# A gated mix of a long convolution and a 2-D spectral filter: the first and last FFT stages in 64x64 and 64x32 tiles, a load to contiguous partitions, the convolution's buffers in another place

## The chip, the cores and the metric

One core of one Trainium2 chip runs the kernel. The metric is the time of one execution on the device in microseconds (us), lower is better. Below, PE is TensorE, DVE VectorE, ACT ScalarE, POOL GpSimd, and SP the engine whose queue issues every DMA of this kernel.

## The reference

```python
def _A_ref(u, log_A_real, A_imag, C_real, C_imag, log_dt, D_skip):   # L = 2048, D = 640, N = 128
    dt = jnp.exp(log_dt)
    A = -jnp.exp(log_A_real) + 1j * A_imag
    C = (C_real + 1j * C_imag) * dt[:, None]
    P = jnp.exp((A * dt[:, None])[:, :, None] * pos[None, None, :])
    K = 2.0 * jnp.einsum("dn,dnl->dl", C, P).real
    y = irfft(rfft(u_t, 2 * L) * rfft(K, 2 * L), 2 * L)[:, :, :L]     # along l
    return y + u * D_skip

def _B_ref(x, w_r, w_i):
    return irfft2(rfft2(x) * (w_r + 1j * w_i))                       # over l and d

g = sigmoid((x * gate_w).sum(-1))
return g * _A_ref(x, ...) + (1 - g) * _B_ref(x, ...)
```

The input u is 2048 x 640 in float32, one batch. Each of the 640 channels has its own response K of 2048 samples, made from 128 modes. The output is float32.

## The kernel before

All transforms are matrix products. The transform along l of a column of channels is split in two: stage 1 (`stage1`) works on groups of four channels and is followed by a twiddled stage 2 (`stage2`) over pairs of frequency rows. The 640 channels go in four column groups c of 160. The program has these parts, each with a tag that the planner sees:

- **params** (tag P): small loads, bf16 splits of the modes' parameters on DVE and POOL, stored to `pp_d` and `pm_d` in DRAM.
- **columns** (A): for each c, stage 1 of u (L626, 8 matmuls a block, four groups q; evicted by ACT, L627), the gate's dot products (L678), stage 2 (L636), copies alternately on ACT and DVE (L689), a store to `u_d` in DRAM.
- **responses** (K): 40 blocks of 16 channels; magnitudes (L890, Exp L891), phases (L902, Sin L903), products on POOL (L912) and DVE (L917, L918, twice L920), a sum over modes on PE (L933) and a store to `k_d`.
- **spectral** (F): nine steps over pairs of rows of `u_d`: transposes and products for the transform along d, the filter's products on DVE (L792 to L802), the way back (L811 to L828), a store to `s3e_d`.
- **convolution** (C): for each c, `first` (stage 1 of `k_d`, L626/L627 again), then nine units: stage 2 (L636), products with u (DVE, L986 to L989; u loaded in L1045), the inverse matmuls (L997), a copy (ACT, L999 or L1003) and a store to `s3_d` (L1000, L1004). Then `even` loads te from `s3e_d` (L1010) and `last` loads t3 from `s3_d` (L1024); each has six rounds of short matmuls (L1015, L1031) with evictions of 128x160 that apply the gate (ACT L1017, DVE L1033); the output is stored in two halves (L1035).

A matmul of the program is two MATMUL rows in the trace, since the data are float32.

The program is not issued in the order of the code. Every call is recorded as a unit of a `Plan`; the rows from first to last access of the buffers give the dependences; `order` then simulates the engines with costs per unit (`occ`, `lag`, a DMA rate, a price for a change of PE's tile shape or of ACT's table) and picks on each engine by rank (time to the end of the program, plus a bias by tag, `OPT`). The list that comes out is emitted as it stands. All SBUF buffers are slices of a single tile `sb` and all PSUM buffers are banks of a single tile `ps`, so the semaphores are derived from overlaps of access patterns within these two tiles. `Space` hands out places: from `T.left` on (the responses') and from `T.right` on (the columns', then the filter's). The convolution's working buffers stand in the filter's place. `Banks` hands out PSUM banks in turn.

The t3 load writes each of its four pieces to every fourth partition:

```python
        for y in range(4):
            src = T.s3_d[c, 16 * y:16 * y + 16].rearrange("k (j x a) d -> (k j) x a d", x=2, j=2)
            Y.dma_start(t3[y::4], src, reads=[("s", c, y)] + [("r33", c)] * (y == 2))
```

## Time and profile before

| | |
|---|---|
| median of three runs | 655.2 us (653.47 to 656.76) |
| the profiled execution | 656.0 us, span 654.2 us |
| PE busy | 531.0 us, 81% of the span |
| PE weight loads busy (beside PE) | 373.3 us, 57% |
| DVE busy | 397.9 us, 61% |
| ACT busy | 350.3 us, 54% |
| POOL busy | 178.9 us, 27% |
| moved by DMA | 100.51 MB, mean 154 GB/s |
| mean granted clock of PE | 0.898 |

A row of a profile's view names engine, line, operation, `out<-in` and shapes (partitions x elements, `xN` for N instructions); in brackets stands the idle time ahead of it and what ended it. A row of the waits reads: engine, line, waited for what, then us in total, times, longest. SPq is the queue on SP on which a DMA is issued. The busy times are averages over parts that have different limits, so they are read by stretches of time.

### The profile page before, as it was taken

Reading aid. Unit: us, or ns where it says so; the run is one execution under the profiler, and the core shown is the slowest. Engines: PE = TensorE matmul, PEld = TensorE weight load, DVE = VectorE, ACT = ScalarE, POOL = GpSimd, SP = SyncE. Lnnn points to the kernel's source line nnn. Section 1 sums busy time; section 2 is a strip of 40 time slices with the busy share of each in tenths; the row PEclk is TensorE's granted clock in tenths of the full one; section 3 lists DMA queues with packets and bytes.
Section 4 is the critical chain, followed back from the end, with each engine's and each line's share of the span. In section 5 each row is a group of like instructions: output and inputs, shape, how many; then the busy total and the mean of one; then the engine's idle time right before and its main releaser. Section 6 shows DMA issues by size and latency. Waiting matters only on the chain.

```text
span 654.2 us, 18460 instructions
## 1 busy us (share of the span) xinstructions
PE 531.0 (81%) x7956; PEld 373.3 (57%) x7956; DVE 397.9 (61%) x724; ACT 350.3 (54%) x572; POOL 178.9 (27%) x159
## 2 busy tenths in 40 slices
PE   7578999788989789898999989928669679469354
PEld 7476986466556556666665647817547457345110
...
GB/s 317 303 146 182 217 174 244 153 90 90 106 78 142 99 154 20 139 66 58 58 50 170 225 80 127 316 151 96 208 80 284 258 149 228 215 153 187 214 40 80
DMA packets 54041, 100.51 MB, mean 154 GB/s; under 512 B 4484, under 2 KB 38024, under 8 KB 52680
## 3 DMA queue, kind: packets, MB, share of 16 engines
...
HBM read 60.00 MB, written 39.32 MB: 152 GB/s over the span
## 4 chain that ended last, share of the span: by engine, by line
PE 46%; DVE 25%; DMA 11%; ACT 7%; issue 4%; SPq 1%; POOL 0%; DVEq 0%; ACTq 0%
PE ps L636 11%; PE ps L626 8%; DMA sb<-s_d 7%; PE ps L997 5%; DMA sb<-u_d 5%; PE ps L1015 4%; PE ps L902 4%; DVE sb L920 4%; PE ps L933 3%; PE ps L726 3%; PE ps L1031 3%; ACT sb L891 2%; DVE sb L918 2%; DVE sb L917 2%; PE ps L827 2%
## 5 line engine op out<-in xcount | busy, mean ns | idle before, releaser
L912 POOL TENSOR_TENSOR sb<-sb 128x512 f32<-128x512 f32 x80 | 108.9, 1387 | 100.4 <-ACT sb L903 96.2
L636 PE MATMUL ps<-sb 128*64 128x160 f32 x1056 | 96.5, 326 | 31.6 <-DMA sb<-s_d 16.3
L636 PEld LDWEIGHTS ps<-sb 128*64 128x64 f32 x1056 | 79.7, 144 | 50.5 <-issue 14.5
L626 PE MATMUL ps<-sb 128*64 128x128 f32 x1280 | 88.4, 289 | 5.5 <-DMA sb<-in_t_c 3.8
L626 PEld LDWEIGHTS ps<-sb 128*64 128x64 f32 x1280 | 77.7, 145 | 14.8 <-issue 5.4
L902 PE MATMUL ps<-sb 52*128 52x512 bf16 x480 | 72.4, 395 | 13.0 <-ACT sb L903 6.8
L627 ACT COPY sb<-ps 128x512 f32<-128x512 f32 x80 | 53.6, 673 | 47.1 <-PE ps L626 47.1
L986 DVE TENSOR_TENSOR sb<-ps,sb 128x640 f32<-128x640 f32 (+1 forms) x36 | 28.3, 785 | 74.0 <-PE ps L636 44.1
L1015 PE MATMUL ps<-sb 128*64 128x480 f32 (+1 forms) x96 | 30.5, 716 | 46.8 <-DMA sb<-s_d 41.8
L891 ACT ACTIVATE sb<-ps 128x1024 f32<-128x1024 f32 (+1 forms) x80 | 62.5, 830 | 5.3 <-PE ps L890 5.0
L999 ACT COPY sb<-ps 128x640 f32<-128x640 f32 x32 | 22.3, 695 | 77.0 <-DMA sb<-s_d 35.9
L689 DVE COPY sb<-ps 128x320 f32<-128x320 f32 x32 | 15.5, 489 | 61.6 <-PE ps L636 39.8
L903 ACT ACTIVATE ps<-ps 128x1024 f32<-128x1024 f32 x40 | 40.5, 1012 | 21.7 <-PE ps L902 11.9
L920 DVE TENSOR_TENSOR sb<-sb,ps 128x512 f32<-128x512 f32 x80 | 51.0, 678 | 0.0
L726 PE MATMUL ps<-sb 128*128 128x161 f32 (+3 forms) x280 | 48.6, 316 | 1.5 <-DVE sb L814 1.5
L997 PE MATMUL ps<-sb 64*64 64x160 f32 x1056 | 49.2, 319 | 0.5 <-DVE sb L988 0.5
L902 PEld LDWEIGHTS <-sb 52*128 52x128 bf16 x480 | 24.1, 97 | 41.2 <-issue 28.5
L903 ACT ACTIVATE sb<-ps 128x1024 f32<-128x1024 f32 x40 | 41.3, 1033 | 11.2 <-PE ps L902 11.1
L997 PEld LDWEIGHTS ps<-sb 64*64 64x64 f32 x1056 | 37.6, 141 | 16.3 <-issue 10.2
L726 PEld LDWEIGHTS ps<-sb 128*128 128x128 f32 (+1 forms) x280 | 39.9, 190 | 11.9 <-issue 8.0
L1033 DVE SCALAR_TENSOR_TENSOR sb<-ps,sb 128x160 f32<-128x160 f32 x64 | 20.8, 377 | 41.2 <-issue 27.8
L917 DVE SCALAR_TENSOR_TENSOR sb<-sb,ps 128x512 f32<-128x512 f32 x40 | 27.3, 683 | 30.5 <-ACT ps L903 30.3
...
## 6 DMA issues: line engine op xcount, KB each, us to landing
...
```

The source lines that it names most:

```text
L626: T.P.matmul(p[64 * ri:64 * ri + 64, j, :], src(i + j), e1[ri], start=True, stop=True)
L627: copy(t1v[:, 4 * (q0 + i):4 * (q0 + i) + 16], p.rearrange("p q (j x y) -> p (q j) x y", j=4, y=2))
L636: T.P.matmul(p[64 * j:64 * j + 64, i, 160 * ri:160 * ri + 160], T.w2[:, x, 64 * ri:64 * ri + 64], t1[:, x // 2 if x < 32 else K0 // 2, :, ...
L726: P.matmul(p[:, 161 * i:161 * i + n], lhs(i, part), tab(i)[part][0], start=i == 0, stop=False)
L891: u = S.activation(ef[:, :, c:c + n], p[:, :, :n], AF.Exp)
L902: P.matmul(p[:, h, :], st.pp[l, zz], turns[l, v, s], start=s == 0, stop=s == 2)
L903: u = S.activation(p if o is None else o, p if o is None else p.rearrange("p h (v c) -> p h v c", v=2), AF.Sin, scale=TWO_PI)
L912: G.tensor_tensor(out=y[:, v], in0=e[:, :, 64:96], in1=sc[:, 1 - v], op=ALU.mult)
L917: V.scalar_tensor_tensor(out=xh[:, 1, :, :, 32:64], in0=eh[:, :, :, 32:64], scalar=-1.0, in1=pv[:, 0], op0=ALU.mult, op1=ALU.mult)
L920: V.tensor_tensor(out=xh[:, 0, h].rearrange("p d (y j) -> p d y j", y=2), in0=eh[:, h, :, 0:64].rearrange("p d (y j) -> p d y j", y=2), in ...
L997: P.matmul(q[x:x + 64, j, 160 * i:160 * i + 160], w3[l, pr + i, ri, x:x + 64], t2[l, ri, i, :], start=ri + i == 0, stop=ri == 1 and i == n ...
L1015: P.matmul(p[i:i + 64], T.e3e[:, i:i + 64], te[:, a:a + n], start=True, stop=True)
```

## The change

- **Stage 1** goes from 128x64 tiles of PE to four 64x64 tiles: the table e1 is cut into two 64-row halves without the zeros between them; eight groups q make a block of 32 matmuls of 64 columns into a pair of banks, and two evictions of 128x512. In the columns these are one on ACT and one on DVE, in the convolution both on ACT. The two halves of a column are 24 and 16 groups (`HALVES`).
- **The last stages** go to eight 64x32 tiles: a round is eight matmuls into a pair of banks, and `even` and `last` have three rounds each (three, three and two rows), with six or four evictions of 128x160. They are one generator `final(c)`.
- **t3** is loaded to contiguous partitions, in six pieces (two of 640 KB, four of 320 KB). The load of te has its source's rows in another order, four groups of 32 where there were 128 rows in a row. The output has another layout, two stores of 640 KB for each c, both after the last round; the host's function turns it back.
- **Places**: the convolution's working buffers stand in the responses' place; te, t3, the even rows and the output, and a second set of u and s3 buffers (used from c = 2), stand in the filter's. PSUM: the inverse and stage 2 have a pair of banks each for c = 0 and 1, later the stage 2 has two pairs. `first(c + 1)` and `final(c - 1)` are interleaved with the units of c in the code.
- **The planner** has other costs for DMAs, for small matmuls and for a change of tile shape, and biases by tag in `OPT`.

The lines behind it are numbered differently: L626 becomes L632, L636 L645, L689 L701, L917/L918/L920 L931/L932/L934, L986 to L989 L998 to L1001, L997 L1009, L999 L1011, L1000 L1012, L1010 L1036, both L1015 and L1031 L1028, L1017 L1038, L1024 L1042, L1033 L1045, L1035 L1047, L1045 L1063.

```diff
-OPT = {}
+OPT = {"bias": {"K": -40e3, "A": 3500.0, "P": 30e3, "C": -40e3}, "hold": 600.0, "table": 1000.0, "slack": {"SP": 300.0, "POOL": 0.0, "PE": 300.0}}
...
-                u = plan.unit(name, {"SP": 60, "ACT": 60, "POOL": 600}[name], 0)
+                u = plan.unit(name, {"SP": 500, "ACT": 500, "POOL": 1200}[name], 0)
...
-    sw, tl = opt.get("switch", 90.0), 1294.0
+    sw, tl = opt.get("switch", 160.0), 1294.0
...
+HALVES = ((0, 24), (24, 16))
...
-        T.e1 = [take(128), take(128)]
-        T.e3, T.e3e, T.id, T.one = take(64), take(128), take(128), take(32)
+        T.e1 = [take(64), take(64)]
+        T.e3, T.e3e, T.id, T.one = take(32), take(64), take(128), take(32)
...
-def stage1(T, bank, e1, src, q0, nq, t1, copy):
-
-    t1v = t1.rearrange("p x d y -> p d x y")
-    for i in range(0, nq, 4):
-        p = bank().rearrange("p (q x) -> p q x", q=4)
+def stage1(T, pair, src, q0, nq, t1, copies):
+
+    t1v = t1.rearrange("p x (q h) y -> p h q x y", h=2)
+    for i in range(0, nq, 8):
+        n = min(8, nq - i)
+        p = pair()
         with block(T.R):
-            for j in range(4):
+            for j in range(n):
                 for ri in range(2):
-                    T.P.matmul(p[64 * ri:64 * ri + 64, j, :], src(i + j), e1[ri], start=True, stop=True)
-        copy(t1v[:, 4 * (q0 + i):4 * (q0 + i) + 16], p.rearrange("p q (j x y) -> p (q j) x y", j=4, y=2))
+                    for h in range(2):
+                        l = slice(64 * h, 64 * h + 64)
+                        T.P.matmul(p[64 * ri:64 * ri + 64, h, 64 * j:64 * j + 64], src(i + j)[l], T.e1[ri][l], start=True, stop=True)
+        for h in range(2):
+            q = 2 * (q0 + i)
+            copies[h](t1v[:, h, q:q + 2 * n], p[:, h, 0:64 * n].rearrange("p (q x y) -> p q x y", x=16, y=2))
+        yield
...
-    bank = Banks(R, [0, 1, 2])
+    wide = Banks(R, [0, 3], 2), Banks(R, [0], 2)
+    slim = Banks(R, [2, 5, 6, 7]), Banks(R, [2, 0, 1])
...
+        pair, bank = wide[c // 2], slim[c // 2]
+        for h, (q0, n) in enumerate(HALVES):
...
-            stage1(T, bank, T.e1, lambda q: u[:, q, :], 20 * h, 20, t1, S.copy)
+                Y.dma_start(T.us[-1][:, 0:n], A["u_l"][c + 1, :, q0:q0 + n])
+            zz = T.az()[:, 0:n]
+            G.tensor_tensor(out=zz, in0=T.one.unsqueeze(1).broadcast_to([128, n, 32]),
+                            in1=T.gw[:, c, q0:q0 + n].unsqueeze(2).broadcast_to([128, n, 32]), op=ALU.mult)
+            for _ in stage1(T, pair, lambda q: u[:, q, :], q0, n, t1, (S.copy, V.tensor_copy)):
+                pass
...
 def convolution(T, A, out):
     R, V, G, S, P, Y = T.R, T.V, T.G, T.S, T.P, T.Y
+    z = Space(R, T.left)
+    kp, t1p, w3p = z.pool(2, 24, 64), z.pool(2, 16, 160, 2), z.pool(1, 17, 2, 128)
+    up, wk, t2p, s3p = z.pool(2, 4, 2, 160), z.pool(4, 2, 2, 160), z.pool(2, 2, 2, 160), z.pool(2, 2, 2, 160)
+    assert z.at <= T.right
     z = Space(R, T.right)
-    kp, t1p, w3p = z.pool(2, 20, 64), z.pool(1, 16, 160, 2), z.pool(1, 17, 2, 128)
-    up, wk, t2p, s3p = z.pool(2, 4, 2, 160), z.pool(4, 2, 2, 160), z.pool(2, 2, 2, 160), z.pool(2, 2, 2, 160)
-    z = Space(R, T.left)
-    t1q = z.pool(1, 16, 160, 2)
-    t1p.bases += t1q.bases
-    oep, tep, t3p, otp = z.pool(2, 16, 160), z.pool(1, 16, 160), z.pool(1, 2, 16, 160), z.pool(2, 8, 160)
-    for pool, more in ((up, z.pool(2, 4, 2, 160)), (s3p, z.pool(2, 2, 2, 160))):
-        pool.bases += more.bases
-    b1, b2, bi, bl = Banks(R, [0]), Banks(R, [1, 3], 2), Banks(R, [5], 2), Banks(R, [7])
+    oep, tep, t3p, otp = z.pool(2, 2, 8, 160), z.pool(1, 16, 160), z.pool(1, 2, 16, 160), z.pool(2, 2, 8, 160)
+    more = (up, z.pool(2, 4, 2, 160)), (s3p, z.pool(2, 2, 2, 160))
+    fin = Banks(R, [0], 2)
+    rings = [(Banks(R, [5], 2), Banks(R, [3], 2))] * 2 + [(Banks(R, [6], 2), Banks(R, [2, 4], 2))] * 2
     w3 = w3p()
     for x in range(2):
         Y.dma_start(w3.rearrange("p k r m -> p (k r m)")[:, 2176 * x:2176 * x + 2176], A["t_w3c"][:, 2176 * x:2176 * x + 2176])
     S.activation(T.gate[:, 1, :], T.gate[:, 0, :], AF.Sigmoid, scale=-1.0)
     S.activation(T.gate[:, 0, :], T.gate[:, 0, :], AF.Sigmoid)
-    def first(c):
-        t1 = t1p()
-        for h in range(2):
+    def first(c, t1):
+        for q0, n in HALVES:
             kt = kp()
-            Y.dma_start(kt, T.k_d[c, :, 20 * h:20 * h + 20], reads=[("k", c, q) for q in range(5 * h, 5 * h + 5)])
-            stage1(T, b1, T.e1, lambda q: kt[:, q, :], 20 * h, 20, t1, S.copy)
-        return t1
+            Y.dma_start(kt[:, 0:n], T.k_d[c, :, q0:q0 + n], reads=[("k", c, q) for q in range(q0 // 4, (q0 + n) // 4)])
+            yield from stage1(T, fin if c > 2 else rings[c][0], lambda q: kt[:, q, :], q0, n, t1, (S.copy, S.copy))
     def unit(c, t1, pr, us):
         n = min(2, 17 - pr)
         nl = 128 if pr < 16 else 64
+        bi, b2 = rings[c]
         p = b2()
         with block(R):
             for i in range(n):
...
             S.copy(s3[:, 0, 0], q[:, 0, 0:160])
             Y.dma_start(T.s3_d[c, 33], s3[0:64, 0, 0, :], writes=[("r33", c)])
-    AS = ((0, 3), (3, 3), (6, 2), (8, 3), (11, 3), (14, 2))
-
-    def even(c):
+    AS = ((0, 3), (3, 3), (6, 2))
+
+    def finish(src, w, take):
+        for a, n in AS:
+            p = fin()[:, :, 0:160 * n].rearrange("p j (a d) -> p j a d", a=n)
+            with block(R):
+                for s in range(2):
+                    for x in range(2):
+                        for j in range(2):
+                            l, o = slice(64 * j, 64 * j + 64), 64 * x + 32 * s
+                            P.matmul(p[o:o + 32, j], w(l, x), src(l, x, 8 * s + a, n), start=True, stop=True)
+            for j in range(2):
+                for i in range(n):
+                    take(j, a + i, p[:, j, i])
+            yield
+
+    def final(c):
         te, oe = tep(), oep()
-        Y.dma_start(te, T.s3e_d[c].rearrange("k (r a) d -> (k r) a d", r=4), reads=[("e", k) for k in range(16)] + [("e1",)])
-        for a, n in AS:
-            p = bl()[:, 0:160 * n].rearrange("p (a d) -> p a d", a=n)
-            with block(R):
-                for i in (0, 64):
-                    P.matmul(p[i:i + 64], T.e3e[:, i:i + 64], te[:, a:a + n], start=True, stop=True)
-            for j in range(n):
-                S.activation(oe[:, a + j], p[:, j], AF.Copy, scale=T.gate[:, 1, a + j:a + j + 1])
-        return oe
-
-    def last(c, oe):
-        t3 = t3p()
-        for y in range(4):
-            src = T.s3_d[c, 16 * y:16 * y + 16].rearrange("k (j x a) d -> (k j) x a d", x=2, j=2)
-            Y.dma_start(t3[y::4], src, reads=[("s", c, y)] + [("r33", c)] * (y == 2))
-        for k, (a, n) in enumerate(AS):
-            if k % 3 == 0:
-                ot = otp()
-            p = bl()[:, 0:160 * n].rearrange("p (a d) -> p a d", a=n)
-            with block(R):
-                for x in range(2):
-                    P.matmul(p[64 * x:64 * x + 64], T.e3, t3[:, x, a:a + n], start=True, stop=True)
-            for j in range(n):
-                V.scalar_tensor_tensor(out=ot[:, a % 8 + j], in0=p[:, j], scalar=T.gate[:, 0, a + j:a + j + 1], in1=oe[:, a + j], op0=ALU.mult, op1=ALU.add)
-            if k % 3 == 2:
-                Y.dma_start(out[c, :, a - 6:a + 2], ot)
-
-    t1 = first(0)
+        Y.dma_start(te.rearrange("p a d -> p (a d)"), T.s3e_d[c].rearrange("k (r a) d -> r k (a d)", r=4), reads=[("e", k) for k in range(16)] + [("e1",)])
+        yield from finish(lambda l, x, a, n: te[l, a:a + n], lambda l, x: T.e3e[l, 32 * x:32 * x + 32],
+                          lambda j, a, p: S.activation(oe[:, j, a], p, AF.Copy, scale=T.gate[:, 1, 8 * j + a:8 * j + a + 1]))
+        t3, ot = t3p(), otp()
+        for k0, k1, ys in ((0, 32, (0, 1)), (32, 48, (2,)), (48, 64, (3,))):
+            for j in range(2):
+                Y.dma_start(t3[64 * j + k0:64 * j + k1].rearrange("p x a d -> p (x a) d"), T.s3_d[c, k0:k1, 32 * j:32 * j + 32],
+                            reads=[("s", c, y) for y in ys] + [("r33", c)] * (k0 == 32))
+        yield from finish(lambda l, x, a, n: t3[l, x, a:a + n], lambda l, x: T.e3[l],
+                          lambda j, a, p: V.scalar_tensor_tensor(out=ot[:, j, a], in0=p, scalar=T.gate[:, 0, 8 * j + a:8 * j + a + 1], in1=oe[:, j, a], op0=ALU.mult, op1=ALU.add))
+        for j in range(2):
+            Y.dma_start(out[c, j], ot[:, j])
+
+    t1 = [t1p() for _ in range(4)]
+    for _ in first(0, t1[0]):
+        pass
     for c in range(4):
-        nxt = first(c + 1) if c < 3 else None
-        us = {}
+        if c == 2:
+            for pool, x in more:
+                pool.bases = pool.bases + x.bases
+        side = [first(c + 1, t1[c + 1])] if c < 3 else []
+        if c:
+            side.append(final(c - 1))
         for g in (0, 4, 8, 16, 12):
             gn = min(4, 17 - g)
             nl = 128 if g < 16 else 64
...
             Y.dma_start(u[:nl, 0:gn], T.u_d[c, :nl, g:g + gn], reads=[("u", c, g + i) for i in range(gn)])
             for pr in range(g, g + gn, 2):
                 n = min(2, g + gn - pr)
-                unit(c, t1, pr, u[:nl, pr - g:pr - g + n])
-        oe = even(c)
-        last(c, oe)
-        t1 = nxt
+                unit(c, t1[c], pr, u[:nl, pr - g:pr - g + n])
+                for x in side:
+                    next(x, None)
+        for x in side:
+            for _ in x:
+                pass
+    for _ in final(3):
+        pass
```

Three places in the order of the instructions. First, DVE about the end of the columns (L689 is the copy behind stage 2, L693 the gate's sum that stands behind the last dot product, L743 the first operation of the filter). Before:

```order
L689 COPY sb<-ps 128x320 x9
L693 TENSOR_REDUCE sb<-sb 128x64
L689 COPY sb<-ps 128x320 x7
L917 SCALAR_TENSOR_TENSOR sb<-sb,ps 128x16x32
L918 TENSOR_TENSOR sb<-sb,ps 128x16x32
L920 TENSOR_TENSOR sb<-sb,ps 128x512 x2
L698 COPY sb<-ps 32x16 x4
L743 TENSOR_TENSOR sb<-sb 128x640
```

After (L635 is a stage 1 eviction, L952 belongs to a finished pair of responses):

```order
L635 COPY sb<-ps 128x16x16x2
L701 COPY sb<-ps 128x320
L931 SCALAR_TENSOR_TENSOR sb<-sb,ps 128x16x32
L932 TENSOR_TENSOR sb<-sb,ps 128x16x32
L934 TENSOR_TENSOR sb<-sb,ps 128x512 x2
L635 COPY sb<-ps 128x16x16x2 x2
L701 COPY sb<-ps 128x320 x2
L705 TENSOR_REDUCE sb<-sb 128x64
L952 TENSOR_TENSOR sb<-sb 128x8
L701 COPY sb<-ps 128x320 x2
```

Before, one response (of 40) stands on DVE ahead of the filter's first operation; after, responses are woven into the columns, and eight are done there. At the other end of the filter, ten responses stood behind the last L801 on DVE before, and none stands behind the last L815 (the same operation) after.

Second, SP's queue at the end of the program, with the semaphores that each DMA waits for (DMAHW names are other DMAs). Before:

```order
L1024 DMA sb<-s_d 32x5120 [waits DVE_49,DMAHW4_49,PE_49,Activation_49]
L1024 DMA sb<-s_d 32x5120 [waits DMAHW7_49,DMAHW5_49]
L1024 DMA sb<-s_d 32x5120 [waits DMAHW2_49,DMAHW1_49]
L1035 DMA out<-sb 128x1280 [waits DVE_49]
L1000 DMA s_d<-sb 128x4x160 [waits DMAHW0_49]
L1024 DMA sb<-s_d 32x5120 [waits DMAHW3_49,DMAHW0_49,PE_49]
L1035 DMA out<-sb 128x1280 [waits DVE_49] x2
```

After:

```order
L1042 DMA sb<-s_d 32x5120 [waits DMAHW2_49,DMAHW3_49,DMAHW1_49,PE_49]
L1042 DMA sb<-s_d 32x5120 [waits PE_49]
L1042 DMA sb<-s_d 16x5120 [waits DMAHW7_49,DMAHW6_49]
L1042 DMA sb<-s_d 16x5120
L1012 DMA s_d<-sb 128x4x160 [waits DMAHW5_49,Activation_49]
L1047 DMA out<-sb 128x1280 [waits DVE_49] x2
L1042 DMA sb<-s_d 16x5120 [waits DMAHW5_49,DMAHW0_49]
L1042 DMA sb<-s_d 16x5120 [waits DMAHW1_49]
L1047 DMA out<-sb 128x1280 [waits DMAHW2_49,DVE_49]
L1047 DMA out<-sb 128x1280 [waits DMAHW3_49,DVE_49]
```

The t3 load no longer waits for DVE and ACT, and its pieces of 16 partitions come last.

Third, PE at the end. Before:

```order
L997 MATMUL ps<-sb 64x160 x16
L1031 MATMUL ps<-sb 64x320 x2
L1015 MATMUL ps<-sb 64x480 x4
L1015 MATMUL ps<-sb 64x320 x2
L1015 MATMUL ps<-sb 64x480 x4
L1015 MATMUL ps<-sb 64x320 x2
L1031 MATMUL ps<-sb 64x480 x4
```

After (L1028 is the matmul of both last stages):

```order
L1009 MATMUL ps<-sb 64x160 x16
L1028 MATMUL ps<-sb 32x320 x8
L1028 MATMUL ps<-sb 32x480 x16
L1028 MATMUL ps<-sb 32x320 x8
L1028 MATMUL ps<-sb 32x480 x16
L1028 MATMUL ps<-sb 32x320 x8
```

Behind the last inverse stood one round of column 2 and twelve of column 3; after, one and six.

More of the change, by code (lines that the diff above doesn't have):

```diff
@@ L55, in _tables @@
     kr[K0, 1] = co[32]
-    e1 = np.zeros((2, 4, 32, 4, 32))
-    for r in range(4):
-        e1[:, r, :, JR[r], :] = kr[:32].transpose(1, 2, 0)
-    e1 = e1.reshape(2, 128, 128)
+    e1 = np.zeros((2, 2, 2, 32, 2, 32))
+    for r in range(2):
+        e1[:, :, r, :, r, :] = kr[:32].transpose(1, 2, 0)[:, None]
+    e1 = e1.reshape(2, 128, 64)
     kr = kr[:32].reshape(64, 32)
-    e3 = np.zeros((64, 2, 2, 32))
-    for j in range(2):
-        e3[:, j, j, :] = kr
-    e3e = np.zeros((32, 4, 4, 32))
-    for r in range(4):
-        e3e[:, r, JR[r], :] = kr[32:64]
+    e3 = np.tile(kr, (2, 1))
+    e3e = np.zeros((2, 2, 32, 2, 32))
+    for x in range(2):
+        e3e[:, x, :, x, :] = kr[32:64]
     one = np.tile(np.eye(32), (4, 1))
     c1 = np.concatenate([
-        e1[0], e1[1], e3.reshape(4, 32, 64).swapaxes(0, 1).reshape(128, 64), e3e.reshape(128, 128), np.eye(128), one,
+        e1[0], e1[1], e3, e3e.reshape(128, 64), np.eye(128), one,
         np.repeat([-1.0, 1.0], 64)[:, None], np.repeat([1.0, -1.0], 64)[:, None],
@@ L292, in call @@
                 else:
-                    t = max(40, a[2].free_size() * 4 / 2.4 * rows * cols / 16384)
+                    t = max(20, a[2].free_size() * 4 / 2.4 * rows * cols / 16384)
                 u.occ += t
@@ L298, in call @@
                 if name == "ACT":
-                    fix = 143 if any(isinstance(k.get(x), AP) for x in ("scale", "bias")) else 39 if op == "copy" else 52
+                    fix = 155 if any(isinstance(k.get(x), AP) for x in ("scale", "bias")) else 42 if op == "copy" else 60
                     u = plan.unit(name, 0.833 * n + fix, 115)
@@ L328, in order @@
             follow[v].append(u)
-    land = lambda u: u.occ + u.lag if u.size is None else u.occ + 2100 + u.size / 330.0
+    land = lambda u: u.occ + u.lag if u.size is None else u.occ + 1300 + u.size / 300.0
+    near = {"DVE": 120, "ACT": 115, "POOL": 0, "PE": 0, "SP": 0}
+    for u in units:
+        u.cost = 45.0 if u.eng == "PE" and any(v.eng != "PE" for v in u.pre) else 0.0
     for u in reversed(units):
-        u.tail = max((v.tail + (u.occ if v.eng == u.eng and u.size is None else land(u) + LAT[v.eng]) for v in follow[u]), default=land(u))
+        u.tail = max((v.tail + (u.occ + near[u.eng] if v.eng == u.eng and u.size is None else land(u) + LAT[v.eng]) for v in follow[u]), default=land(u))
     bias = opt.get("bias", {})
@@ L376, in order @@
             if u.mode != mode:
-                s += sw / 2
+                s = max(s, free[e] + sw)
                 mode = u.mode
-                free[e] = s + u.occ + sw / 2
             else:
-                free[e] = s + u.occ
+                s = max(s, free[e] + u.cost)
+            free[e] = s + u.occ
         elif u.table and u.table != table:
@@ L392, in order @@
         if u.size is not None:
-            dma = max(dma, s + u.occ) + u.size / opt.get("bw", 330.0)
-            done = dma + 2100
+            dma = max(dma, s + u.occ + 700) + u.size / opt.get("bw", 300.0)
+            done = dma + 450
         out.append(u)
         for v in follow[u]:
-            t = s + u.occ if v.eng == e and u.size is None else done + LAT[v.eng]
+            t = s + u.occ + near[e] if v.eng == e and u.size is None else done + LAT[v.eng]
             est[v] = max(est[v], t)
@@ L500, in body @@
         R.tag = "A"
-        Y.dma_start(c1[:, 0:256], A["t_c1"][:, 0:256])
+        Y.dma_start(c1[:, 0:128], A["t_c1"][:, 0:128])
         columns_head(T, A)
-        Y.dma_start(c1[:, 256:nc1], A["t_c1"][:, 256:nc1])
+        Y.dma_start(c1[:, 128:nc1], A["t_c1"][:, 128:nc1])
         R.tag = "P"
@@ L668, in columns @@
                 T.us.append(T.au())
-                Y.dma_start(T.us[-1], A["u_l"][c + 1, :, 20 * h:20 * h + 20])
-            zz = T.az()
-            G.tensor_tensor(out=zz, in0=T.one.unsqueeze(1).broadcast_to([128, 20, 32]),
-                            in1=T.gw[:, c, 20 * h:20 * h + 20].unsqueeze(2).broadcast_to([128, 20, 32]), op=ALU.mult)
-            stage1(T, bank, T.e1, lambda q: u[:, q, :], 20 * h, 20, t1, S.copy)
+                Y.dma_start(T.us[-1][:, 0:n], A["u_l"][c + 1, :, q0:q0 + n])
[4 more added lines that the diff above has]
+                pass
             p = bank()[:, 0:64]
             with block(R):
-                for q in range(20):
+                for q in range(n):
                     x = 32 * (q % 4)
-                    P.matmul(p[x:x + 32], zz[:, q, :], u[:, q, :], start=q < 4, stop=q > 15)
+                    P.matmul(p[x:x + 32], zz[:, q, :], u[:, q, :], start=q < 4, stop=q >= n - 4)
             S.copy(T.lg[:, 2 * c + h, :], p)
@@ L696, in columns @@
             P.matmul(p[32 * r:32 * r + 32], T.one, T.lr, start=True, stop=True)
-    for r, x in enumerate((slice(31, 15, -1), slice(32, 48), slice(15, None, -1), slice(48, 64))):
-        V.tensor_copy(T.gate[32 * r:32 * r + 32, 0, :], p[32 * r:32 * r + 32, x])
+    for r in range(4):
+        l, a = slice(32 * r, 32 * r + 32), 8 * r
+        V.tensor_copy(T.gate[l, 0, 0:8], p[l, 31 - a:23 - a if r < 3 else None:-1])
+        V.tensor_copy(T.gate[l, 0, 8:16], p[l, 32 + a:40 + a])
 def spectral(T, A):
@@ L1037, in convolution @@
-    t1 = first(0)
-    for c in range(4):
-        nxt = first(c + 1) if c < 3 else None
-        us = {}
+    AS = ((0, 3), (3, 3), (6, 2))
[4 more added lines that the diff above has]
+                for s in range(2):
+                    for x in range(2):
+                        for j in range(2):
[5 more added lines that the diff above has]
+            yield
```

21 lines of the change are left out of this document (10 added, 11 removed).

## The prediction

> **What bounds the kernel now.** I read the stages first: the busy time of each engine in the stretches params and columns (to 120), responses beside the filter (to 400), convolution (to 607), end. The last row is the first 20 us alone. The columns are stretch, PE, PEld, DVE, ACT, POOL, granted clock, DMA share, GB/s.
>
> ```profile
> 0.00:120.00 120.00, 98.32 (x1549) 84.86 (x1551) 52.71 (x93) 61.18 (x107) 34.84 (x31) 0.92 0.65 227
> 120.00:340.00 220.00, 199.97 (x3075) 133.30 (x3075) 207.20 (x350) 171.25 (x262) 115.84 (x106) 0.98 0.28 87
> 340.00:400.00 60.00, 55.24 (x988) 35.23 (x978) 33.93 (x67) 49.78 (x73) 28.14 (x23) 0.97 0.48 156
> 400.00:421.00 21.00, 21.00 (x466) 17.99 (x466) 16.36 (x30) 10.05 (x13) 0.07 (x1) 1.00 0.77 259
> 421.00:607.00 186.00, 135.52 (x1858) 98.25 (x1852) 81.81 (x169) 52.12 (x103) 0.00 (x0) 0.84 0.57 184
> 607.00:655.00 48.00, 20.90 (x52) 3.66 (x51) 5.89 (x18) 5.92 (x17) 0.00 (x0) 0.53 0.29 103
> 0.00:20.00 20.00, 16.13 (x282) 15.49 (x284) 1.15 (x3) 9.15 (x16) 5.21 (x8) 1.00 0.92 331
> ```
>
> Up to 340 DVE is the bound, 207 of 220 us; from 340 to 400 it is PE, 55 of 60. From 400 to 421 PE is never idle; after 421 it is busy 136 of 186 us and no other engine is busier, so something stops them all. The waits of 400 to 607 (us in total, times, longest) and the chain there say what:
>
> ```profile
> DVE sb L986 <- PE ps L636: 44.1, 21, 6.1
> ACT sb L999 <- DMA sb<-s_d: 35.9, 4, 13.0
> PE ps L1015 <- DMA sb<-s_d: 32.3, 3, 13.5
> DVE sb L989 <- DMA sb<-s_d: 30.9, 3, 14.0
> DVE sb L986 <- DMA sb<-s_d: 28.3, 3, 12.7
> ```
> ```profile
> by line: PE ps L636 17.1%; PE ps L997 16.8%; DMA sb<-s_d 16.7%; DMA sb<-u_d 11.3%; PE ps L626 10.5%; PE ps L1015 8.2%; PE ps L1031 4.2%; DVE sb L987 3.5%; DVE sb L986 3.0%; DVE sb L1033 2.1%; SPq L1024 1.7%; issue 1.6%; PE ps L933 1.1%; DVE
> 421.19 6.52 DMA sb<-u_d
> 427.79 4.17 DMA sb<-s_d
> ```
>
> ACT's copy L999 and DVE's products L986 and L989 don't read what the t3 load (sb<-s_d, L1024) brings, yet they wait for it, three or four times each, up to 14 us; and t3 itself waits for the u load before it. On the chain of these 207 us the t3 loads are 16.7% and the u loads 11.3%, 58.0 us. The first stop:
>
> ```profile
> 423.73 1.33 PE L997 MATMUL ps<-sb 64*64 64x160 f32 x32
> 432.11 0.69 ACT L999 COPY sb<-ps 128x640 f32<-128x640 f32 x1 [8.58 <-DMA sb<-s_d]
> 432.14 0.82 DVE L986 TENSOR_TENSOR sb<-ps,sb 128x640 f32<-128x640 f32 x1 [10.18 <-DMA sb<-s_d]
> ```
>
> ACT and DVE go on within 0.03 us of each other. The last unit ends at 607; what follows is a chain of loads and short rounds:
>
> ```profile
> 607.04 0.69 ACT L999 COPY sb<-ps 128x640 f32<-128x640 f32 x1 [3.61 <-PE ps L997]
> 617.12 1.87 PE L1015 MATMUL ps<-sb 128*64 128x480 f32 x4 [9.49 <-DMA sb<-s_d]
> 619.02 0.96 ACT L1017 ACTIVATE sb<-ps,sb 128x160 f32<-128x160 f32 x3 [11.28 <-PE ps L1015]
> 634.19 1.87 PE L1031 MATMUL ps<-sb 128*64 128x480 f32 x4 [1.91 <-DMA sb<-s_d]
> 649.49 0.68 DVE L1033 SCALAR_TENSOR_TENSOR sb<-ps,sb 128x160 f32<-128x160 f32 x2 [1.44 <-PE ps L1031]
> ```
>
> PE stands for 9.5 us, and then each round (matmul, evictions, matmul, ...) is in series: 17 us of L1015, 17 of L1031, the output's landing.
>
> **The change, part by part.** The sum is made against the profiled execution's own span, 654.2 us (656.0 with what lies around it, 0.8 above the median of 655.2).
>
> *The hand-over to the convolution* now stands at its first product:
>
> ```profile
> 400.81 0.82 DVE L986 TENSOR_TENSOR sb<-ps,sb 128x640 f32<-128x640 f32 x1
> L917 DVE SCALAR_TENSOR_TENSOR sb<-sb,ps 128x512 f32<-128x512 f32 x40 | 27.3, 683 | 30.5 <-ACT ps L903 30.3
> L918 DVE TENSOR_TENSOR sb<-sb,ps 128x512 f32<-128x512 f32 x40 | 27.1, 678 | 0.0
> L920 DVE TENSOR_TENSOR sb<-sb,ps 128x512 f32<-128x512 f32 x80 | 51.0, 678 | 0.0
> L902 PE MATMUL ps<-sb 52*128 52x512 bf16 x480 | 72.4, 395 | 13.0 <-ACT sb L903 6.8
> L933 PE MATMUL ps<-sb 128*32 128x64 f32 x2560 | 45.0, 221 | 0.9 <-POOL sb L912 0.6 <-issue 0.4
> ```
>
> A response costs DVE 0.683 + 3 x 0.678 = 2.72 us and PE at least (72.4 + 45.0)/40 = 2.9. In the new order eight of the 40 are done on DVE in the columns, where DVE was busy 53 of 120 us, against one. So 7 x 2.72 = 19 us leave the stretch behind: 207.2 + 33.9 - 19 = 222, and at the pace of 120 to 340 (207.2/220) that is 236 us, not 280. Against this: the params' loads (2.56 MB) go ahead of the first u load on SP, 7.7 us at 331 GB/s; the columns' PE loses about 20 us of stage 1 and gains 7 x 2.9 = 20; I let the filter begin 5 us later. All responses are now done ahead of the last filter step, so its own chain of PE, DVE and POOL lies bare: 10 us (estimate; DVE was idle 26 of the 60 us in 340 to 400). The loads of w3, k and u for the convolution, now with places of their own, are 4.8 MB, 14.5 us at 331 GB/s, half of it covered: 8. 120 + 5 + 236 + 10 + 8 = 379, so **-22** (-33 if hole and loads are covered and the filter starts on time; -6 if the hole is 26).
>
> *The t3 load.* Contiguous partitions end the false waits: in the built program the new load holds up only the last stage's matmuls, and waits for the stores that it reads and for the matmuls that free its place. Of the 58.0 us I take 40 as gone: the t3 part, 34.6, whole, and little of the u part, since u loads still come through the same queue: **-40** (-35 to -58).
>
> *First stage.* A block of 16 rows stood at 1.09 us between other work, in a run at 4.59/5 = 0.92:
>
> ```profile
> 398.25 1.09 PE L626 MATMUL ps<-sb 128*64 128x128 f32 x16
> 72.17 4.59 PE L626 MATMUL ps<-sb 128*64 128x128 f32 x80
> 130.16 1.11 PE L933 MATMUL ps<-sb 128*32 128x64 f32 x64
> 423.73 1.03 PEld L997 LDWEIGHTS ps<-sb 64*64 64x64 f32 x32 [0.24 <-ACT sb L627]
> ```
>
> A new block has twice the groups in 64 rows of 64 columns. The nearest matmuls are L933's, 64 rows of 64 columns in 1.11 us; the nearest tile is L997's, whose 32 rows of 160 columns (1280 columns for each of four tiles) took 1.33 us, the same 1.0 ns a column as the 1024 columns for each of two tiles in 1.09, so four 64x64 tiles do work side by side. After 400 some 29 old blocks (31.6 us) become 15 new (16.7): **-15**. The other end is zero: at L997's 1.03/32 us a weight load, 64 loads take 2.06 us, as much as two old blocks.
>
> *Last stages.* Six rounds become three of the same columns in twice the tiles. At full clock:
>
> ```profile
> 589.54 1.03 PE L1015 MATMUL ps<-sb 128*64 128x480 f32 x4
> 592.92 0.76 PE L1015 MATMUL ps<-sb 128*64 128x320 f32 x4
> ```
>
> 36 rounds (24 x 1.03 + 12 x 0.76 = 33.8 us) of the body become 18: **-17** (0 if the eight tiles work four at a time). The evictions stay 16 of 128x160 on the same engines, beside other work. Some 11 more changes of tile shape in the convolution at the 0.24 us that stood ahead of L997 above: **+3**.
>
> *What is given back in the body.* Units of column 0 and 1 have one stage 2 pair of banks where two alternated, so the next unit's matmuls wait for L986 and L987 (0.8 us each, beside an inverse of 1.33 us): 18 units that may lose up to 1.1 us, **+8** (0 to +20). And the same 39.7 MB go through in 160 us, 248 GB/s where the fullest stretch had 331 at a DMA share of 0.92, so loads queue: **+14** (0 to +25). The body, 400.8 to 606.9: -40 - 15 - 17 + 3 + 8 + 14 = **-47**, 206 to 159 us (the ends add to -12 and -78; PE's own work, about 129 us, is the floor).
>
> *The end.* After the last inverse now stand one round of column 2 and three + three of column 3, still at half clock (0.53). A round of three rows: 1.87 us of matmuls and six evictions (2 x 0.96), and the single pair of banks makes these serial, so some 3.9; of two rows 1.33 + 1.4. That is 1.3 + 2 x 10.5 = 22, then two output loads of 640 KB where one was (4.7 us from the last eviction to the span's end): 6, and 2 us of starts: 30.5 against 47.3, **-16** (-6 to -22). The t3 load is hidden under the even rows' three rounds: in the trace the last loads start right behind the copy of 607.04 and release PE at 617.12, some 9.4 us; the rounds ahead take 11.8.
>
> *At nothing:* the evictions split to ACT and DVE in the columns (DVE busy 53 of 120), the gate's extra four copies, the 24/16 halves.
>
> Sum: -22 - 47 - 16 = -85, span 569, executed 571, median **571** within its spread.
>
> **The rivals.**
> *The te load on few engines.* The even rows' load (L1010, 1.31 MB) had 128 rows on both sides; its source is now four groups of 32. If the queue spreads a load by its outermost count, four DMA engines carry it: 331/0.92/16 = 22.5 GB/s each, 14.6 us where 16 take 3.6, and all that is queued behind on those four is late by 11 us. Four loads, half of it hidden by units: +22, **593** (615 with none hidden). The trace has no load with such a source, neither for nor against. The Trainium skill, DMA: Bandwidth & Descriptors, section "Why a DMA increments its semaphore by 16 and not by 1", states such a rule: the engines used are the largest number up to 16 that divides the outermost counts of both sides. By that rule it is four here; no trace of this case shows it yet.
>
> *Small tiles no faster.* Weight loads bound stage 1 (2.06 us a block) and eight tiles go four at a time: -15 and -17 vanish, the rounds at the end double (+10), the columns keep their time (+7): **620**. Against it: L997's columns above.
>
> *All chain waits vanish,* loads hidden: -58 in place of -40, +14 and +8 gone: **531 to 545**. Against it: u and s loads still share one queue and 39.7 MB.
>
> *Slower:* the te load comes down to one engine, 58 us each at 22.5 GB/s, in front of t3 and u on SP. Four such loads pay back the 85 us once each holds up the chain for more than 21 us; wholly exposed, 4 x 55 more, **790**, half hidden 680. For it: nothing but that the shape is untried; against it: the outer count is four.
>
> **How the numbers follow.** 0.52 for the forecast (its own ends 552 to 592), 0.29 for te on four engines, 0.08 for the small tiles, 0.08 for all waits gone, 0.03 for slower. The range 540 to 613 holds all of the first two but their edges. Within 0.5% (3.3 us), about what a measurement of this kernel can tell from no change, needs mishaps that add to 85: 0.02; faster 0.95, slower 0.03.
>
> **What would show it.** Right: no ACT or DVE wait on sb<-s_d; stage 1 blocks of 64 rows near 1.1 us; rounds of 16 rows near 1.0 at full clock; the first convolution product near 379; the end near 30 us behind the last inverse; te landing some 4 us after issue. Wrong: te landing at 14 us or more with the units behind it waiting (second rival); 2 us blocks (third); a first product after 390, or DVE waiting for stage 2 throughout columns 0 and 1, would break the first or the given-back terms.

## The result, and the profile after

The changed kernel takes 653.8 us (median of 20 runs, 648.5 to 664.6) against 656.1 before: a ratio of 0.994 (0.991 to 0.997). Executions fall into a faster and a slower state; the ratios, and the times of the experiments, are those of the faster one. The change gains 0.6%, where 571 us and a range of 540 to 613 were forecast. The profiled execution has a span of 648.5 us. Its stages, with the columns of the table before (stretch, PE, PEld, DVE, ACT, POOL, granted clock, DMA share, GB/s); the last three rows are the convolution's body, first product to last inverse, of before and of after, and the end of after:

```profile
120.00:340.00 220.00, 201.06 (x3083) 135.25 (x3081) 204.37 (x351) 175.06 (x263) 119.19 (x107) 0.97 0.32 101
400.00:421.00 21.00, 8.69 (x228) 6.75 (x217) 5.84 (x10) 3.64 (x5) 0.00 (x0) 0.82 0.57 170
421.00:607.00 186.00, 121.64 (x2396) 83.73 (x2396) 81.36 (x166) 53.58 (x105) 0.00 (x0) 0.83 0.69 173
400.80:607.00 206.20, 155.72 (x2304) 115.45 (x2302) 97.37 (x197) 62.17 (x115) 0.00 (x0) 0.86 0.60 192
386.00:599.00 213.00, 140.27 (x2807) 98.64 (x2806) 95.04 (x187) 60.29 (x115) 0.00 (x0) 0.84 0.70 178
599.00:649.00 50.00, 16.16 (x112) 2.46 (x110) 6.58 (x22) 5.58 (x17) 0.00 (x0) 0.56 0.53 129
```

PE has 15 us less to do in the body, and the body is 7 us longer. PE is idle there for 73 us; between 400 and 421, where it never stood still before, it works 9 of 21. The first product comes at 386.2 (400.8 before, 379 forecast), and the end still takes 50 us (47 before, 30 forecast). The waits and the longest stop say what took the place of the t3 load:

```profile
ACT sb L1011 <- DMA s_d<-sb: 68.8, 8, 25.5
PE ps L632 <- ACT sb L1011: 32.5, 4, 18.9
DVE sb L998 <- DMA sb<-u_d: 22.9, 2, 21.4
```
```profile
436.42 0.57 SPq L1036 DMA_DIRECT2D sb<-s3e_d  x1
...
442.83 0.38 SPq L1012 DMA_DIRECT2D s_d<-sb  x1
...
447.79 23.20 SPq L1012 DMA_DIRECT2D s_d<-sb  x2
...
469.91 0.69 ACT L1011 COPY sb<-ps 128x640 f32<-128x640 f32 x1 [25.45 <-DMA s_d<-sb]
470.65 1.98 PE L632 MATMUL ps<-sb 64*64 64x64 f32 x64 [18.95 <-ACT sb L1011]
471.71 0.82 DVE L998 TENSOR_TENSOR sb<-ps,sb 128x640 f32<-128x640 f32 x1 [21.43 <-DMA sb<-u_d]
...
530.54 16.55 SPq L1063 DMA_DIRECT2D sb<-u_d  x2
```
```profile
460.00:468.00 8.00, 0.00 (x0) 0.00 (x0) 0.00 (x0) 0.00 (x0) 0.00 (x0) 0.50 0.25 76
```

No unit waits for t3 any more. ACT's copy L1011 waits for the stores of s to land and free its buffers, 68.8 us in eight stops. In the stop shown, the te load (L1036) was issued at 436.42; by the trace's DMA records its packets ran from 440.9 to 466.6, and the store that the copy waits for was issued behind it, at 442.83. PE stands behind the copy, and DVE waits for a u load. SP's queue stands too: of the 23.2 us of the two stores at 447.79 the first issue takes 5.6 us, and then the queue waits 17.2 us for ACT's copy. The longest single issue is the first of the two u loads at 530.54, 16.1 us, again behind a te load. In eight microseconds of the stop no engine works and the DMA share is 0.25, as much as 4 of 16 DMA engines (the last row).

### The profile page after: what moved, and what is told of

It is laid out like the page before. It is cut to its first block, busy times and chain, and to the rows that moved or that the text cites. A ratio compares the mean times of both kernels' runs of the same rounds, so it can differ in the third digit from the quotient of the medians.

```text
span 648.5 us, 21440 instructions
## 1 busy us (share of the span) xinstructions
PE 495.0 (76%) x9428; PEld 340.0 (52%) x9428; DVE 412.3 (64%) x748; ACT 336.8 (52%) x552; POOL 183.4 (28%) x159
## 5 line engine op out<-in xcount | busy, mean ns | idle before, releaser
L645 PE MATMUL ps<-sb 128*64 128x160 f32 x1056 | 97.4, 320 | 17.1 <-DVE sb L999 8.3
L632 PE MATMUL ps<-sb 64*64 64x64 f32 x2560 | 55.4, 244 | 51.6 <-ACT sb L1011 32.5
L645 PEld LDWEIGHTS ps<-sb 128*64 128x64 f32 x1056 | 74.0, 139 | 37.4 <-DVE sb L999 13.5
L632 PEld LDWEIGHTS ps<-sb 64*64 64x64 f32 x2560 | 49.9, 156 | 62.1 <-ACT sb L1011 35.3
L1011 ACT COPY sb<-ps 128x640 f32<-128x640 f32 x32 | 22.3, 697 | 108.4 <-DMA s_d<-sb 68.8
L1009 PE MATMUL ps<-sb 64*64 64x160 f32 x1056 | 54.6, 326 | 25.6 <-ACT sb L1011 20.3
L635 ACT COPY sb<-ps 128x512 f32<-128x512 f32 x60 | 42.7, 776 | 50.8 <-PE ps L632 50.3
L998 DVE TENSOR_TENSOR sb<-ps,sb 128x640 f32<-128x640 f32 (+1 forms) x36 | 28.2, 784 | 61.1 <-PE ps L645 38.1
L1009 PEld LDWEIGHTS ps<-sb 64*64 64x64 f32 x1056 | 40.2, 145 | 43.4 <-ACT sb L1011 26.4
L1028 PE MATMUL ps<-sb 64*32 64x480 f32 (+1 forms) x384 | 38.1, 667 | 30.8 <-DMA sb<-s3e_d 14.0
L917 ACT ACTIVATE ps<-ps 128x1024 f32<-128x1024 f32 x40 | 40.4, 1010 | 24.0 <-PE ps L916 16.5
L1045 DVE SCALAR_TENSOR_TENSOR sb<-ps,sb 128x160 f32<-128x160 f32 x64 | 19.9, 376 | 50.3 <-issue 33.5
L934 DVE TENSOR_TENSOR sb<-sb,ps 128x512 f32<-128x512 f32 x80 | 51.1, 679 | 0.0
L740 PE MATMUL ps<-sb 128*128 128x161 f32 (+3 forms) x280 | 50.4, 325 | 0.0
L740 PEld LDWEIGHTS ps<-sb 128*128 128x128 f32 (+1 forms) x280 | 41.4, 197 | 11.7 <-issue 6.5
L917 ACT ACTIVATE sb<-ps 128x1024 f32<-128x1024 f32 x40 | 41.3, 1034 | 9.5 <-PE ps L916 9.0
L1000 DVE TENSOR_TENSOR sb<-sb 128x320 f32<-128x320 f32 (+1 forms) x36 | 16.8, 467 | 44.6 <-PE ps L1009 44.4
L947 PE MATMUL ps<-sb 128*32 128x64 f32 x2560 | 43.8, 220 | 0.0
```

The costliest lines, as they stand in the source:

```text
L632: T.P.matmul(p[64 * ri:64 * ri + 64, h, 64 * j:64 * j + 64], src(i + j)[l], T.e1[ri][l], start=True, stop=True)
L635: copies[h](t1v[:, h, q:q + 2 * n], p[:, h, 0:64 * n].rearrange("p (q x y) -> p q x y", x=16, y=2))
L645: T.P.matmul(p[64 * j:64 * j + 64, i, 160 * ri:160 * ri + 160], T.w2[:, x, 64 * ri:64 * ri + 64], t1[:, x // 2 if x < 32 else K0 // 2, :, ...
L740: P.matmul(p[:, 161 * i:161 * i + n], lhs(i, part), tab(i)[part][0], start=i == 0, stop=False)
L917: u = S.activation(p if o is None else o, p if o is None else p.rearrange("p h (v c) -> p h v c", v=2), AF.Sin, scale=TWO_PI)
L934: V.tensor_tensor(out=xh[:, 0, h].rearrange("p d (y j) -> p d y j", y=2), in0=eh[:, h, :, 0:64].rearrange("p d (y j) -> p d y j", y=2), in ...
```

## The experiments

Ratios are against the kernel before on the same chip (656 to 659 us); intervals are 95%.

**te: in four, in two groups, and in the kernel before.** In te_four each te load is four loads of 32 partitions at the same place of the queue:

```diff
-        Y.dma_start(te..., T.s3e_d[c].rearrange("k (r a) d -> r k (a d)", r=4), ...)
+        for r in range(4):
+            Y.dma_start(te[32 * r:32 * r + 32]..., T.s3e_d[c, :, 16 * r:16 * r + 16].rearrange("k a d -> k (a d)"), ...)
```

te_two has two loads `te[64 * r:64 * r + 64]` from `"k (r a) d -> r k (a d)", r=2`. before_te_groups gives only the new source, `"k (r a) d -> r k (a d)"`, to the kernel before. All other instructions keep their order in all three.

> The changed kernel with the te load cut into four loads of 32 partitions (same place in the queue, same order of everything else). Theory A, te was carried by four DMA engines and what queued behind it on them (stores of s, loads of u) stopped the units: the stretches with a DMA share near 0.25 vanish, ACT's copy L1011 no longer waits 10 to 25 us for s_d stores, and the time falls from 654 to 570 to 595. Theory B, the volume of transfers or the two s buffers stop the units: the stops stay and the time is above 635.

> The changed kernel with te in two loads of 64 partitions, whose source has two groups outside instead of four. Theory A (the outermost count sets the number of engines): two engines, a DMA share near 0.13 in the stops, and each te about twice as long (some 30 us alone), so four times 15 to 25 us more: 710 to 750. Theory B: no change within 10 us of 654.

> The kernel before with nothing changed but the te load's source, in four groups of 32 rows (the even rows' result is then of other rows). Theory A: each te takes 15 us or more on four engines and delays t3 and u behind it: 655 becomes 690 to 730. Theory B: within 1% of 655.

te_four: 607.3 us, 0.925 (0.921 to 0.929). te_two: 695.3, 1.059 (1.050 to 1.069). before_te_groups: 714.8, 1.089 (1.085 to 1.094). The first row is the wait of te_four that was 68.8 above, the other two are stretches within stops of te_two:

```profile
ACT sb L1011 <- DMA s_d<-sb: 24.7, 6, 8.1
```
```profile
420.00:428.00 8.00, 0.00 (x0) 0.00 (x0) 0.00 (x0) 0.00 (x0) 0.00 (x0) 0.50 0.13 54
645.00:650.00 5.00, 0.00 (x0) 0.00 (x0) 0.00 (x0) 0.00 (x0) 0.00 (x0) 0.50 0.13 53
```

The dose answers: four groups outside give a share of 0.25, two give 0.13, 32 give no such stop. From its first to its last packet a te load takes 21 to 26 us with four groups (the changed kernel), 28 to 38 with two, 7 to 10 in te_four and 5 to 7 in the kernel before. Against te_four, four groups cost some 46 us (653.8 to 607.3) and two cost 88 (695.3, less than the 710 to 750 expected); in the kernel before, four cost 59. Theory A holds. The Trainium skill, DMA: Bandwidth & Descriptors, section "Why a DMA increments its semaphore by 16 and not by 1", has the rule (the largest number up to 16 that divides both outermost counts), and the trace agrees with it. te_four missed its range of 570 to 595, so more was wrong.

**The t3 load alone.** The kernel before, with `t3[32 * y:32 * y + 32]` for `t3[y::4]` and e3's rows in the matching order (`e3.reshape(128, 64)`); the same order on all engines.

> The kernel before with nothing changed but the t3 load, to contiguous partitions (the rows of the table e3 in the matching order). If the false waits on t3 are worth what the prediction put on them, 40 us go: 610 to 622. If other waits stand right behind them, the time is 635 to 650.

589.8 us, 0.900 (0.895 to 0.904): 66 us, better than the whole change, and more than the 40 forecast. Its body (first row) and end:

```profile
402.00:548.00 146.00, 142.39 (x2316) 107.35 (x2312) 98.05 (x198) 62.72 (x116) 0.00 (x0) 1.00 0.90 272
548.00:588.00 40.00, 15.92 (x50) 2.99 (x48) 5.90 (x18) 5.49 (x17) 0.00 (x0) 0.66 0.44 123
```

PE is busy 142 of 146 us, and for the same matmuls it needs 13 us less than before (155.7): it no longer stops, and its granted clock is 1.00, not 0.86. So a stop costs its own length and then some clock. The changed kernel shows it at one stop: in the idle stretch from 460 to 468 the granted clock was 0.50, and the block of stage 1 behind it (470.65) took 1.98 us, where another run's block took 1.16 (row 60.18 below). With the t3 load settled, the rest of the change, without the te load, costs 17 us (589.8 to 607.3).

**The planner's part.** t3_planner is before_t3_contiguous with the new costs and biases; te_four_oldplan is te_four with those of before.

> The kernel before with the contiguous t3 load and the new planner (costs, biases), old tiles and places. te_four with all the rest of the change is 17 us slower than the contiguous t3 load alone (607 against 590). If the planner's order is what costs (theory P), this one is 600 to 610 as well. If the order is good by itself (responses into the columns, first product earlier by 15 us as in te_four), it is 570 to 582.

> te_four with the planner of before (costs, no biases), new tiles and places. Theory P: 590 or less. If tiles and places cost and the planner gains, it is 615 to 630.

626.8 us, 0.953 (0.948 to 0.957), and 642.8, 0.975 (0.970 to 0.979): neither theory. By the ratios the new order costs 35 us on the old tiles and gains 33 on the new ones, so an order fits the kernel that it was set for. In t3_planner the first product comes at 375, but responses then run on beside the convolution: DVE has 123 us in the body, not 98, and the body is 210 us long.

```profile
375.00:585.00 210.00, 189.22 (x3105) 130.47 (x3103) 123.45 (x240) 104.98 (x164) 25.43 (x20) 0.91 0.65 196
```

**Buffers, and t3 in pieces of 16 partitions.** In te_four_early `if c == 2:` for the second buffers becomes `if c == 1:`, and `rings` has its first entry once, its second three times. In te_four_t3 the pieces `(0, 32, (0, 1)), (32, 48, (2,)), (48, 64, (3,))` become `(0, 32, (0, 1)), (32, 64, (2, 3))`. t3_pieces16 goes the other way: in before_t3_contiguous each piece is two loads of 16 partitions.

> te_four with the second pair of u and s buffers and the two pairs of banks for stage 2 from column 1 on instead of column 2. Theory B (two s buffers and one pair of banks hold the units of columns 0 and 1, where ACT's copy waits for stores): one of these two columns is freed, 607 becomes 594 to 600. Otherwise it stays within 4 us of 607.

> te_four with t3 in pieces of 32 partitions only (four a column in place of two of 32 and four of 16). In the trace's DMA records a 20480-byte packet of t3 took 0.97 us to partitions a stride apart, 1.4 us to 32 contiguous partitions and 2.2 us to 16. Theory D (the transfers' own time is the bound, because few contiguous partitions take data slowly): 16 packets a DMA engine come down from 2.2 to 1.4 us, 12 us less, 594 to 600. Otherwise 603 to 611.

> The kernel before with contiguous t3 in eight pieces of 16 partitions a column in place of four of 32, all else in the same order. Theory D (few contiguous partitions take data slowly): 32 packets a DMA engine go from 1.4 to 2.2 us, 25 us more transfer time; the convolution there has PE busy 141 of 145 us and a DMA share of 0.91, so the transfers become the bound and 590 becomes 600 to 612. If the packets' times in the other runs came from what else was under way, it stays at 588 to 594.

te_four_early: 635.2, 0.963 (0.957 to 0.969); its body is 9 us shorter than te_four's (169 against 178), but the first product comes at 411 instead of 386, and the end is 55 us. So it tells nothing clear of theory B. te_four_t3: 592.5, 0.902 (0.896 to 0.908); the planner's list is also another one there. t3_pieces16: 616.9, 0.939 (0.936 to 0.943), with all other instructions in the same order: by the ratios 26 us more for the same bytes. Mean durations of the t3 packets (20480 bytes each, 512 a run), from the trace's DMA records:

```
kernel                  partitions of a piece     mean us   the last 32 of the run
before                  32, every fourth          0.98      0.89
before_t3_contiguous    32 in a row               1.46      1.36
te_four_t3              32 in a row               1.48      1.51
te_four                 32 and 16 in a row        1.75      2.26 (pieces of 16)
t3_pieces16             16 in a row               2.32      2.02
```

Theory D holds: at the end of the run, with little else under way, the three kinds stand in the same order (0.89, 1.36 to 1.51, 2.02 to 2.26). The Trainium skill, SBUF — State Buffer, section "Door 1: The DMA port swizzle (why `[64,N]` ≈ `[32,N]`)", has it as the number of the 16 ports that the partitions reach. By its table that is 16 for every fourth partition, 8 for 32 in a row and 4 for 16 in a row; the three durations go that way. The body of te_four_t3 and its end:

```profile
384.00:539.00 155.00, 128.98 (x2778) 93.28 (x2774) 91.35 (x176) 59.97 (x115) 0.00 (x0) 0.97 0.81 226
539.00:589.00 50.00, 24.55 (x151) 3.65 (x144) 9.89 (x32) 5.57 (x17) 0.00 (x0) 0.51 0.68 192
```

**The end.** t3_second_place: te_four_t3 with the last column's t3 in the first buffer of t1, no longer used. one_te: that, with the te load for column 0 only. final_on_pool: t3_second_place with te loads and output stores from POOL's queue. out_held: t3_second_place with column 2's output stores behind the last store of s. out_held_te: that, with the last te in a buffer of k.

```diff
-        t3, ot = t3p(), otp()
+        t3, ot = t3p() if c < 3 else Pool(R, [t1p.bases[0]], (2, 16, 160))(), otp()
...
+    for j, ot in held:                                       # out_held: column 2's
+        Y.dma_start(out[2, j], ot[:, j]).pre[stores[3]] = 1
```

> te_four_t3 with a place of its own for the last column's t3 (the first buffer of t1). In te_four_t3 the t3 loads of column 3 waited on SP for the last matmuls of column 2, and the last store of s stood behind them (544 ready, 554 issued). If this is what made the end 49 us where 30 were forecast: 592 becomes 574 to 582. If the transfers' volume made it, it stays within 4 us.

> t3_second_place with the te loads and the output stores issued from POOL's queue, which is idle in the convolution, in place of SP's; the stores of s and the loads of t3 and u on SP no longer stand behind them. If the order on the one queue costs, another 5 to 15 us go; if the transfers themselves are the bound, no change within 4 us.

> t3_second_place with the te load for column 0 only (the other columns use the same rows, 3.9 MB less). If the transfers' time still bounds the convolution, 3 x 32 packets of 0.73 us an engine, 18 us, go in part: 8 to 18 us less than t3_second_place. If PE and its evictions bound it, 0 to 5.

> t3_second_place with the output stores of column 2 held back on SP until the last store of s is issued; the order is otherwise the same. In t3_second_place the copy of the last unit was done at 542.4 and its store issued at 554.2, behind those output stores, which wait for DVE; it then took 8.6 us to land behind their 1.3 MB. If SP's order makes the end long: the store goes out some 8 us earlier and lands some 3 us faster, 594 becomes 582 to 588. If the transfers' volume makes it, the end stays at 50 us and the time within 4 us.

> out_held with a place of its own for the last column's te as well (in the buffers of k, no longer used), so its load needn't wait for column 2's matmuls nor stand on SP ahead of the last stores of s. If SP's order in the last 50 us is what is left, the time falls below out_held by 4 to 10 us; else no change within 4 us, or what the new order of the whole list gives.

t3_second_place: 594.4, 0.906 (0.900 to 0.911), no gain. final_on_pool: 613.5, 0.934 (0.928 to 0.940), worse; in its profiled execution (622.4, 9 us above that) the end takes 35 us, the shortest here, but the first product comes at 399 and the body takes 187. one_te: 576.2 (one of its two runs, the profiled one), against 588.7 to 596.4 for t3_second_place. Its list is another one from the filter on, too: between the two profiled executions (588.7 and 576.2) 5.5 us go ahead of the first product and 5.5 in the body (152.5 to 147.0), where two of the three loads left out had stood. So the transfers' time may bound a part of the body; it is not shown clear of the order. out_held: 589.1, 0.897 (0.894 to 0.900), 6 us by the ratios; out_held_te: 584.0, 0.888 (0.884 to 0.893), the fastest here with all its loads, beating both kernels and, narrowly, the t3 load alone. Here is out_held's end:

```profile
543.12 0.69 ACT L1011 COPY sb<-ps 128x640 f32<-128x640 f32 x1 [6.18 <-DMA s_d<-sb]
...
551.85 0.37 SPq L1012 DMA_DIRECT2D s_d<-sb  x1
554.86 1.77 PE L1028 MATMUL ps<-sb 64*32 64x480 f32 x2 [4.02 <-DMA sb<-s3e_d]
...
560.56 0.79 SPq L1042 DMA_DIRECT2D sb<-s_d  x2
...
567.46 3.74 PE L1028 MATMUL ps<-sb 64*32 64x480 f32 x16 [0.81 <-ACT sb L1038]
571.32 1.84 DVE L1045 SCALAR_TENSOR_TENSOR sb<-ps,sb 128x160 f32<-128x160 f32 x6 [19.14 <-issue]
```

The last column's t3 is now in time (PE waits for ACT at 567.46, not for t3), yet the end is 48 us: nine rounds in series, where seven had been counted, wait in turn for te and for each other's evictions.

**Does PE's time count?** stage1_twice is te_four_t3 with each matmul of the convolution's stage 1 done twice, orders unchanged.

> te_four_t3 with every matmul of the convolution's stage 1 done twice (20 blocks of 64 rows become 128, some 1.0 us more each on PE, 20 us; all orders unchanged). It undoes on PE what the 64x64 tiles saved there. If PE's time is the path of the convolution, 592 becomes 608 to 614. If the transfers and the waits at the single pairs of banks set the pace, PE has room for it: 592 to 600, and the tiles' saving was worth little here.

637.4 us, 0.967 (0.960 to 0.973): by the ratios 42 us, outside both ranges, for 26 us more matmuls of stage 1 (L632 is busy 79.1 us, 53.3 in te_four_t3). PE's time counts, so the saving of the tiles was not idle. The rest are stops of PE with nothing in the profile to wait for:

```profile
PE ps L632 <- issue: 16.7, 7, 5.1
```
```profile
502.32 1.85 PE L632 MATMUL ps<-sb 64*64 64x64 f32 x113
509.31 0.69 PE L632 MATMUL ps<-sb 64*64 64x64 f32 x15 [5.15 <-issue]
```

These two rows are one block of 128, so PE stood in the middle of it. The trace's DMA records say for what. Between 360 and 600 PE has 13 such stops of over 0.3 us, 29.6 us together, and each ends 1.2 to 1.6 us after a packet of 16384 bytes has landed on the queue that the profile calls "instruction" (84 such packets in this run, 74 in te_four_t3). te_four_t3 has five that end like this, 8.5 us; before_t3_contiguous has one, 0.3 us. So PE waited for its own instructions: 21 us more stops and 26 us more matmuls make 47 of the 49 us between the two profiled executions (638.6 and 589.9). The agreement in time is what shows this; no run changed it alone. The body, in which the clock falls to 0.91:

```profile
395.00:588.00 193.00, 151.83 (x3732) 114.23 (x3732) 91.33 (x176) 60.08 (x115) 0.00 (x0) 0.91 0.66 182
```

## Why the prediction was wrong

The forecast was 83 us too low. te_four takes 46 us of it away and te_four_t3 another 15; what is left there, 21 us, is nearly all the end (49 us, 30 forecast). The step that failed first is te: the sum put its load at nothing, landing some 4 us after issue, while its packets took 21 to 26 us and cost 46 us. The other two steps that failed are the time of t3's transfers to contiguous partitions and the order of loads and stores at the end.

- *The te load* stood as a rival with 0.29 and 593 us. Its mechanism was right. In it, "half of it hidden by units" failed: with two s buffers, and with stores, u loads and SP's issues held up behind te, the price was 46 us, not 22. The time of a load was too small as well: 14.6 us were estimated for four engines that carry nothing else, and other transfers shared them.
- *What is given back in the body* priced the transfers by bytes alone. That contiguous partitions slow the t3 load itself was not seen: 0.98 to 1.46 us a packet, and to 2.2 for pieces of 16. t3_pieces16 puts 26 us on it for 32 packets an engine, te_four_t3, in another order, 15 for half as many.
- *The t3 load*, -40 (-35 to -58): alone it is -66. The mechanism was right (the false waits are gone), the term too small: the clock's part was left out (13 us of PE's time), PE behind the stops was free to run without a pause, and 7 us came off the end.
- *First stage*, -15: on PE it came. Body rows of before_t3_contiguous's old blocks and te_four_t3's new ones (the same stretch, those matmuls alone), one block, and one round of the last stages:

```profile
402.00:548.00 146.00, 31.84 (x464) 26.38 (x464) 1.00 0.90 272
384.00:539.00 155.00, 18.13 (x960) 16.21 (x960) 0.97 0.81 226
60.18 1.16 PE L632 MATMUL ps<-sb 64*64 64x64 f32 x64
528.15 1.03 PE L1028 MATMUL ps<-sb 64*32 64x480 f32 x16
```

  31.8 became 18.1 us, at 1.16 for the block shown (1.11 forecast). A round of the last stages is 1.03 us in twice the tiles, as forecast; small tiles that are no faster, the third rival, are out.
- *The hand-over*, -22: -14.6, inside its bounds. The 7 us lie ahead of the filter: its first operation on DVE stands at 131.8 against 121.1, 10.7 us later, where 5 had been let; from there to the first product it took 254 us, as forecast.
- *The order* was counted only for what it moved into the columns. It was worth some 35 us either way, by the tiles that it met; no term or rival spoke of it.
- *The body* in te_four_t3 is 155 us, 159 forecast: with the two transfers mended its sum comes out, but by luck, since t3's gain and the transfers' price were both larger than their terms. Why it isn't below the 145 of before_t3_contiguous, with 13 us less on PE, is only in part shown: 8.5 us are the stops for instructions, which the sum had at nothing, and one_te, in another order, takes it to 147. The 8 us for the single pairs of banks were not measured alone, and the 0.24 us a change of tile shape was read from a wait for ACT.
- *Bounds.* Two don't follow from their terms: the hand-over's -33 (its three conditions are worth 23 us, so -45), and the body's -12 and -78 (the ranges of its terms give -19 and -87 with the tiles' gains kept).
- *The end*, -16: +2. After waits there for te and then for t3:

```profile
614.15 1.86 PE L1028 MATMUL ps<-sb 64*32 64x480 f32 x16 [13.95 <-DMA sb<-s3e_d]
631.57 3.32 PE L1028 MATMUL ps<-sb 64*32 64x480 f32 x16 [8.50 <-DMA sb<-s_d]
636.03 2.73 PE L1028 MATMUL ps<-sb 64*32 64x480 f32 x16 [1.15 <-DVE sb L1045]
```

  The rounds cost what was forecast (636.03 to 639.86 is 3.8 us). "The t3 load is hidden under the even rows' three rounds" failed: te came 13.95 us late, and the last store of s stood on SP behind four t3 loads (600.27 to 616.01), which took 6.7 us to issue the first two and then waited 8.1 us for earlier stores of s. The last two t3 loads, which read that store, went out at 625.59. With te in four loads from SP the end is 40 us in te_four and 44 to 59 in the other orders, with nine rounds in out_held; which part the order has and which the transfers is open.
